# Attention and rational feed-forward: both halves of the first values in one queue, units of 6, 6 and 4 blocks, and a new order

## The chip, the cores and the metric

The kernel runs on one core of a Trainium2 chip. The metric is the device time of one execution in microseconds, taken beside other runs of the same program; three runs of the kernel before gave 272.96 (median), 270.09 and 273.46. Four engines do the work here: PE (TensorE, matrix products), DVE (VectorE), ACT (ScalarE), and POOL (GpSimd, only for constants at the start). SP issues most of the DMAs, ACT issues a few. Each engine takes its instructions strictly in the order in which the program lists them, so a wait at one instruction holds back everything listed behind it on that engine.

## What is computed

The inputs are q, k and v with 4 batches, 4 heads, 1088 positions and 32 values a head, two sketch matrices S1 and S2 of 8 by 32, and the weights of a feed-forward layer of width 2048 on 128 channels. Cut to what matters:

```python
def phi(x):                                   # 64 features from 32 values
    a = einsum('rd,bhsd->bhsr', S1, x)
    b = einsum('rd,bhsd->bhsr', S2, x)
    return einsum('bhsi,bhsj->bhsij', a, b).reshape(*x.shape[:-1], 64)
q_p, k_p = phi(q), phi(k)
kv = einsum('bhsf,bhsd->bhfd', k_p, v)
z = sum(k_p, axis=2)
x = einsum('bhsf,bhfd->bhsd', q_p, kv) / (einsum('bhsf,bhf->bhs', q_p, z)[..., None] + 1e-6)
# heads side by side: 4352 tokens of 128 channels
h = x @ w_in                                  # 4352 x 2048
P = a[0] + a[1]*h + a[2]*h**2 + a[3]*h**3
Q = 1 + abs(b[0])*abs(h) + abs(b[1])*h**2
out = (P / (Q + 1e-6)) @ w_out
```

All of the keys and values of a batch must be summed into kv before any of its queries can be finished, so the first batch's keys and values stand at the head of everything.

## The kernel before

**Attention.** For each batch, the function keys (L416) transposes the keys on DVE (L424, L426), sketches them on PE with S1 and S2 (L444), copies one of the two sketches to SBUF on ACT (L449), multiplies the two into features k_p on DVE (L452) and adds the products of k_p with the values on PE (L463). ACT keeps the sum as kvz (L480). The first batch's keys go through this in five parts of 1, 3, 2, 2 and 1 tiles. A product reads all 128 partitions of the values, which are loaded in two halves of 64 partitions (L289 and L290). The function queries (L494) transposes queries (L503), sketches them (L525 for the first two chunks, which are of 256 positions and called direct, or L553 for the others, called spread), makes features, and multiplies with kvz (L591); then come denominator, inverse and quotient on DVE (L600, L604, L607), a transpose on PE (L613) and a copy into xT on ACT (L620). The sketches of a spread chunk go out to DRAM and come back repeated over partitions (a_all and b_all, L566 to L577), before DVE multiplies them (L561). These small transfers share SP's queue with the loads.

**Feed-forward.** The 4352 tokens are cut into one tile of 256, seven of 512 and two of 256. A tile's 16 blocks of 128 hidden values are worked in units: four units of 4 blocks in the first tile, three units in each tile of 512 (PERS, L160), then units of 8, 8, and of 8, 6 and 2 blocks in the last two. There are 30 units. In each, PE computes h (L672) into one of two PSUM buffers of 1024 columns, and ACT evacuates each buffer (L676). A buffer holds two blocks of 512 tokens, so a unit with an odd number of blocks has one evacuation that is half as wide. Then DVE takes the absolute value u (L684), w = |b1| u + |b0| (DVE L689 or ACT L691) and y = w u (L694). ACT takes the logarithm (L697) and the exponential (L700): r is the inverse of the denominator. DVE makes s = h r (L709). How the polynomial is finished depends on the unit's mode, one digit of MODES (L150) a unit:

- mode 2 makes p = a3 h + a2 (L704 or L706), then h p + a1 (L718, L722 or L724) and g from it (L727); PE gathers 2 terms, r and g;
- mode 3 makes p, h s (L712) and g = p h s (L715); PE gathers 3 terms, r, s and g;
- mode 4 makes h s (L712) and h h s (L730) and no p; PE gathers 4 terms.

Each term is multiplied with a copy of the output weights that is scaled with its coefficient (L400 to L406, from the raw weights in the tile ln), and summed in PSUM (L762). DVE transposes the result (L771) and DMAs store it.

**The order.** Every step of the kernel is created with a number, and the table PLACE (L167) gives the place at which it is emitted; ON_ACT (L220) lists the steps that may run on either engine and run on ACT. Emission in the order of places fixes the order of each engine's queue. FILLS (L224) puts matmuls on idle data ahead of two places at the start. The argument behind of a DMA demands only that its place comes after that of another step; it is no wait on the chip. Buffers in PSUM and SBUF take turns (h two, hh four, r three, s, p and g two each, ln and u one), and DMAs take turns with eight semaphores: a DMA that takes a semaphore again waits first for the DMA that held it before.

**The start.** SP issues S2, the first keys, the values' first half (L289), the rest of the first queries, the two halves of the output weights, the first half of w_in, the second batch's keys and queries. ACT issues S1, the first 256 queries, the values' second half (L290) and two small loads of the vectors b and a (L308). The second half of w_in comes later on SP, between the transfers of the first spread chunk.

Of the kernel before, what the change touches and what calls it, by code (L numbers as in the profile page):

```python
# [20 lines left out]
def kernel(  # L21
# [15 lines left out]
    B, H, S, D = q.shape  # L37
# [3 lines left out]
    nf = d_ff // 128  # L41
# [8 lines left out]
    W = NT * D  # L50
# [74 lines left out]
    def d_four(n, ptr):  # L125
# [24 lines left out]
    MODES = '332423333332433332334442444442'  # L150
# [9 lines left out]
    PERS = (6, 5, 5)  # L160
# [7 lines left out]
        1, 0, 2, 3, 4, 5, 8, 13, 14, 20, 15, 73, 22, 16, 18, 6, 7, 9, 12, 10, 11, 41, 46, 59, 47, 65, 72,  # L168
        56, 82, 75, 51, 81, 85, 97, 17, 19, 24, 27, 29, 32, 21, 25, 31, 38, 26, 30, 35, 44, 33, 37, 39, 49,
        42, 45, 48, 50, 54, 23, 28, 34, 36, 52, 57, 61, 62, 66, 69, 70, 40, 53, 67, 58, 68, 74, 79, 84, 88,  # L170
        103, 111, 76, 80, 86, 87, 90, 91, 43, 60, 63, 71, 64, 89, 94, 83, 129, 132, 137, 141, 146, 149, 152,
        77, 93, 98, 105, 101, 119, 124, 127, 172, 190, 194, 200, 203, 213, 240, 106, 118, 55, 92, 96, 116,
        122, 126, 136, 120, 128, 131, 143, 104, 110, 115, 150, 166, 107, 155, 158, 162, 164, 188, 186, 173,
        216, 222, 228, 234, 237, 241, 244, 117, 176, 177, 210, 184, 218, 211, 215, 257, 263, 277, 283, 294,
        321, 344, 167, 180, 195, 196, 214, 229, 232, 267, 268, 274, 281, 284, 289, 292, 298, 278, 272, 271,
        279, 314, 319, 329, 340, 352, 370, 357, 374, 378, 387, 383, 385, 391, 402, 408, 305, 311, 317, 318,
        324, 342, 337, 338, 390, 421, 424, 428, 441, 445, 454, 347, 350, 353, 358, 356, 361, 359, 360, 407,
        468, 488, 493, 497, 510, 516, 327, 363, 366, 371, 372, 450, 418, 411, 451, 466, 487, 512, 525, 586,
        621, 457, 548, 465, 459, 483, 479, 545, 552, 566, 582, 528, 540, 565, 597, 571, 579, 580, 612, 613,
        481, 535, 539, 541, 546, 556, 561, 590, 616, 623, 626, 627, 638, 647, 654, 536, 568, 576, 588, 581,  # L180
        589, 593, 596, 660, 679, 685, 698, 703, 709, 749, 640, 650, 656, 662, 659, 674, 681, 739, 768, 787,
        793, 795, 820, 838, 840, 78, 99, 102, 108, 113, 114, 123, 134, 100, 148, 151, 135, 142, 156, 95,
        112, 121, 130, 139, 140, 153, 163, 145, 185, 189, 301, 246, 193, 125, 133, 144, 147, 154, 161, 168,
        178, 157, 174, 181, 187, 206, 239, 109, 138, 160, 165, 171, 175, 182, 192, 219, 251, 220, 221, 245,
        261, 331, 464, 431, 422, 420, 159, 170, 179, 191, 169, 183, 198, 201, 204, 212, 227, 243, 199, 209,
        223, 256, 248, 253, 250, 306, 288, 303, 202, 207, 197, 205, 208, 225, 230, 235, 238, 247, 252, 260,
        231, 266, 270, 304, 381, 259, 297, 296, 295, 302, 309, 286, 226, 236, 233, 242, 217, 224, 255, 282,
        285, 290, 299, 308, 264, 316, 323, 313, 312, 326, 325, 320, 328, 332, 335, 330, 400, 401, 410, 417,
        404, 249, 258, 254, 262, 265, 273, 291, 293, 300, 310, 322, 334, 280, 349, 369, 416, 433, 336, 396,
        379, 395, 414, 393, 415, 287, 307, 276, 333, 269, 275, 343, 348, 355, 367, 377, 386, 365, 398, 412,  # L190
        472, 437, 467, 499, 425, 443, 444, 452, 448, 315, 339, 345, 354, 341, 346, 368, 376, 382, 388, 413,
        430, 399, 434, 442, 435, 426, 485, 458, 439, 460, 449, 455, 471, 533, 663, 670, 687, 686, 752, 682,
        741, 691, 351, 362, 364, 375, 373, 384, 394, 406, 419, 429, 440, 469, 456, 477, 491, 555, 506, 482,
        519, 501, 508, 498, 504, 553, 403, 409, 389, 392, 380, 397, 432, 447, 461, 462, 490, 505, 446, 470,
        476, 527, 521, 502, 517, 530, 558, 573, 405, 423, 427, 436, 438, 453, 474, 489, 495, 500, 509, 532,
        598, 608, 549, 547, 611, 551, 538, 560, 618, 645, 646, 624, 617, 622, 649, 668, 669, 657, 653, 475,
        480, 478, 484, 486, 494, 503, 513, 514, 524, 531, 542, 522, 557, 569, 610, 543, 629, 572, 562, 564,
        603, 591, 606, 463, 473, 492, 496, 507, 515, 518, 537, 550, 559, 570, 577, 544, 585, 601, 693, 688,
        689, 609, 592, 602, 651, 643, 671, 526, 554, 511, 520, 523, 529, 575, 583, 594, 599, 630, 631, 607,
        639, 644, 633, 675, 721, 695, 642, 665, 680, 672, 692, 732, 740, 750, 756, 738, 736, 748, 734, 733,  # L200
        563, 578, 534, 567, 584, 587, 605, 614, 620, 634, 635, 664, 661, 677, 678, 655, 720, 754, 683, 711,
        725, 708, 729, 699, 574, 595, 600, 604, 615, 619, 628, 641, 652, 676, 700, 714, 684, 697, 724, 743,
        772, 716, 710, 761, 757, 764, 637, 648, 636, 658, 625, 632, 673, 696, 704, 715, 727, 735, 701, 751,
        762, 771, 742, 766, 746, 745, 782, 818, 808, 773, 825, 905, 897, 834, 909, 702, 706, 666, 690, 705,
        707, 717, 723, 728, 737, 759, 774, 718, 779, 785, 829, 812, 817, 800, 786, 797, 813, 807, 803, 713,
        722, 726, 731, 712, 719, 747, 758, 763, 775, 781, 790, 802, 819, 791, 837, 814, 799, 809, 823, 815,
        832, 824, 836, 831, 844, 730, 753, 744, 755, 667, 694, 769, 778, 784, 792, 801, 810, 835, 854, 822,
        849, 858, 839, 855, 830, 850, 868, 885, 863, 862, 856, 888, 900, 972, 906, 978, 899, 912, 894, 910,
        760, 767, 765, 776, 770, 780, 794, 796, 806, 811, 833, 847, 857, 867, 869, 908, 911, 865, 918, 866,
        892, 927, 896, 873, 880, 878, 783, 788, 777, 789, 804, 805, 826, 827, 841, 848, 859, 874, 843, 852,  # L210
        870, 879, 884, 882, 895, 914, 915, 891, 842, 846, 798, 828, 816, 821, 853, 864, 872, 876, 883, 893,
        903, 916, 919, 938, 944, 907, 917, 931, 939, 933, 942, 947, 923, 948, 960, 969, 980, 964, 970, 851,
        861, 845, 860, 877, 886, 889, 898, 904, 925, 929, 951, 924, 959, 949, 975, 956, 945, 966, 971, 875,
        890, 871, 881, 902, 913, 920, 926, 930, 941, 950, 963, 955, 967, 954, 953, 983, 962, 981, 979, 1002,
        1012, 1017, 1004, 1016, 887, 922, 901, 921, 928, 932, 934, 943, 957, 968, 977, 988, 974, 995, 991,
        1001, 985, 992, 1000, 998, 935, 936, 937, 940, 946, 952, 958, 965, 976, 989, 999, 1009, 984, 990,
# [50 lines left out]
    def flat(x, b):  # L267
        return x[b].rearrange("h (g j) d -> (h g) (j d)", g=32)
# [569 lines left out]
```

## Time and profile before

| | |
|---|---|
| time, median of 3 runs | 272.96 us (270.09 to 273.46) |
| profiled execution: its own time | 272.55 us |
| profiled execution: span from first to last instruction | 270.7 us |
| granted clock of PE, mean | 0.992 |
| busy time of ACT, share of the span | 247.6 us, 91% |
| longest wait of PE for a DMA (L463 for the values) | 2.8 us |
| longest wait of DVE (L452 for the copy L449) | 4.7 us |
| PE's waits for the evacuation L676 | 6.4 us in 13 waits, the longest 0.8 |

The profile comes from one execution. Its span leaves out 1.85 us that the execution's own time holds. A busy time is the time in which an engine had at least one instruction under way; instructions of one engine overlap a little at their ends, so durations add up to more than the busy time. A line of the timeline gives the start, the duration, the engine, the line of the code and the operation, with its output and its inputs, and in brackets how long the engine was idle before it and what released it. "x8" says that eight instructions are merged in the line. A matmul of 32-bit values counts as two instructions.

### The profile page before, as it was taken

The page shows a single profiled execution, that of the slowest core. Times are in us where ns is not written, and L with a number is a line of the kernel's source. Part 1 is how long each engine was busy: PE and PEld are TensorE (multiplying, and loading weights), DVE is VectorE, ACT ScalarE, POOL GpSimd, SP SyncE. Part 2 cuts the span into 40 slices and gives each one's busy share as a digit, 9 for nine tenths or more (in the row PEclk, how much of TensorE's full clock was granted, in tenths as well). Part 3 has the DMA queues.
Part 4 walks back from the last instruction along what each step waited for, and adds up shares of the span by engine and source line. Part 5 has one row for each costly group of instructions (what it writes and reads, how often), then busy time and mean ns, then how long its engine had stood idle before and what let it go on. Part 6 is the DMA issues. An engine that isn't in the chain of part 4 may idle for free.

```text
span 270.7 us, 4291 instructions
## 1 busy us (share of the span) xinstructions
PE 261.4 (97%) x1673; PEld 143.1 (53%) x1673; DVE 254.4 (94%) x301; ACT 247.6 (91%) x217; POOL 2.7 (1%) x25
## 2 busy tenths in 40 slices
PE   8589999999999999999999999999999999999994
PEld 5467755555443454454444554444444446666783
DVE  3389999999999999999999999999999999999993
ACT  1179999999999999999999999999998999999981
POOL 4000000000000000000000000000000000000000
PEclk9799999999999999999999999999999999999999
DMA  5947514599006447600004310430300000020032
GB/s 174 289 190 206 148 31 114 101 181 194 3 17 109 96 65 149 209 1 0 0 17 127 104 58 0 63 94 0 59 11 2 0 11 0 0 42 11 0 58 39
DMA packets 29063, 20.13 MB, mean 74 GB/s; under 512 B 19316, under 2 KB 24948, under 8 KB 29044
## 3 DMA queue, kind: packets, MB, share of 16 engines
q1 hardware_dynamic: 28064, 19.37, 31.0%
q10 hardware_dynamic: 980, 0.49, 0.7%
q8 instruction: 13, 0.21, 0.4%
q14 instruction: 6, 0.05, 0.1%
HBM read 16.65 MB, written 3.21 MB: 73 GB/s over the span
## 4 chain that ended last, share of the span: by engine, by line
PE 59%; ACT 19%; DVE 11%; issue 6%; DMA 3%; ACTq 0%; DVEq 0%
PE h_ps L672 28%; PE out_ps L762 22%; ACT ln L697 6%; ACT r L700 5%; ACT hh L676 4%; DMA v_sb<-in_v_dram 3%; PE att_ps L591 3%; ACT p L706 2%; PE att_ps L463 2%; DVE g L712 2%; PE att_ps L553 1%; PE att_ps L444 1%; DVE w L694 1%; DVE g L715 1%; DVE s L709 1%
## 5 line engine op out<-in xcount | busy, mean ns | idle before, releaser
L672 PE MATMUL h_ps<-xT,w_in_sb 128*128 128x512 f32 (+1 forms) x320 | 129.7, 537 | 0.7 <-ACT hh L676 0.3
L672 PEld LDWEIGHTS h_ps<-xT,w_in_sb 128*128 128x128 f32 x320 | 58.0, 190 | 43.8 <-issue 30.2
L762 PEld LDWEIGHTS <-w_out 128*128 128x128 bf16 x513 | 48.9, 98 | 52.5 <-issue 22.0
L676 ACT CAST hh<-h_ps 128x1024 bf16<-128x1024 f32 (+1 forms) x76 | 69.2, 949 | 1.5 <-PE h_ps L672 1.3
L697 ACT ACTIVATE ln<-w 128x2560 f32<-128x2560 bf16 (+5 forms) x30 | 65.0, 2167 | 1.0 <-DVE w L694 1.0
L700 ACT ACTIVATE r<-ln 128x2560 bf16<-128x2560 f32 (+5 forms) x30 | 65.0, 2166 | 0.4
L709 DVE TENSOR_TENSOR s<-hh,r 128x2560 bf16<-128x2560 bf16 (+5 forms) x30 | 40.8, 1360 | 0.6 <-ACT r L700 0.2
L694 DVE TENSOR_TENSOR w<-w,u 128x2560 bf16<-128x2560 bf16 (+5 forms) x30 | 40.6, 1354 | 0.1
L762 PE MATMUL out_ps<-r,w_out 128*128 128x512 bf16 (+1 forms) x160 | 39.6, 347 | 0.0
L762 PE MATMUL out_ps<-g,w_out 128*128 128x512 bf16 (+1 forms) x160 | 38.6, 347 | 0.0
L762 PE MATMUL out_ps<-s,w_out 128*128 128x512 bf16 (+1 forms) x133 | 32.3, 346 | 0.0
L706 ACT ACTIVATE p<-hh,a_sb 128x2560 bf16<-128x2560 bf16 (+3 forms) x12 | 29.2, 2431 | 0.0
L684 DVE TENSOR_SCALAR u<-hh 128x2560 uint16<-128x2560 uint16 (+5 forms) x30 | 22.7, 756 | 0.8 <-ACT hh L676 0.6
L689 DVE TENSOR_SCALAR w<-u,b_abs 128x2560 bf16<-128x2560 bf16 (+3 forms) x24 | 22.0, 919 | 0.1
L715 DVE TENSOR_TENSOR g<-p,g 128x2560 bf16<-128x2560 bf16 (+2 forms) x14 | 20.5, 1465 | 0.1
L712 DVE TENSOR_TENSOR g<-hh,s 128x2560 bf16<-128x2560 bf16 (+2 forms) x14 | 20.5, 1462 | 0.1
L712 DVE TENSOR_TENSOR p<-hh,s 128x2560 bf16<-128x2560 bf16 (+4 forms) x10 | 13.0, 1299 | 0.1
L730 DVE TENSOR_TENSOR g<-p,hh 128x2560 bf16<-128x2560 bf16 (+4 forms) x10 | 12.9, 1292 | 0.0
L762 PE MATMUL out_ps<-p,w_out 128*128 128x256 bf16 (+1 forms) x60 | 12.9, 319 | 0.0
L591 PEld LDWEIGHTS att_ps<-kvz,a_all 128*64 128x64 f32 x288 | 9.6, 137 | 5.4 <-issue 2.5
L591 PE MATMUL att_ps<-kvz,a_all 128*64 128x66 f32 x288 | 11.2, 225 | 0.6 <-DVE a_all L540 0.3
L691 ACT ACTIVATE w<-u,b_abs 128x1024 bf16<-128x1024 bf16 (+3 forms) x6 | 10.2, 1698 | 0.3 <-DVE u L684 0.3
(78 smaller groups left out, 182.2 us busy)
## 6 DMA issues: line engine op xcount, KB each, us to landing
b_all<-sk_d SPq DMA_DIRECT2D x12, 192.0 KB
a_all<-sk_d SPq DMA_DIRECT2D x6, 384.0 KB
kq<-in_k_dram SPq DMA_DIRECT2D x4, 544.0 KB
kq<-in_q_dram SPq DMA_DIRECT2D x3, 544.0 KB
a_all<-sk_d SPq DMA_DIRECT2D x4, 320.0 KB
b_all<-sk_d SPq DMA_DIRECT2D x8, 160.0 KB
v_sb<-in_v_dram SPq DMA_DIRECT2D x4, 256.0 KB
ln<-in_moe_w_out_dram SPq DMA_DIRECT2D x2, 512.0 KB
```

The costliest lines, as they stand in the source:

```text
L591: nc.tensor.matmul(nd.t[x:x + 64, o:o + 2 * KW], lhsT=(av(c)[:, o0 + x:o0 + x + 64] if how == "direct" else q_p.t[:, c * n + o0 + x:c * n ...
L672: nc.tensor.matmul(h.t[:, (x - x0) * tl:(x - x0 + 1) * tl], lhsT=w_in_sb[:, f * 128:(f + 1) * 128], rhs=xT[:, xpos(t0):xpos(t0) + tl], sta ...
L676: nc.scalar.copy(out=hh.t[:, x0 * tl:x1 * tl], in_=h.t[:, 0:(x1 - x0) * tl])
L684: nc.vector.tensor_scalar(out=u.t[:, :n].bitcast(U16), in0=hh.t[:, :n].bitcast(U16), scalar1=0x7FFF, scalar2=None, op0=AX.bitwise_and)
L694: nc.vector.tensor_mul(out=y.t[:, :n], in0=w.t[:, :n], in1=u.t[:, :n])
L697: nc.scalar.activation(out=ln.t[:, :n], in_=y.t[:, :n], func=ACT.Ln, bias=1.0 + 1e-6)
L700: nc.scalar.activation(out=r.t[:, :n], in_=ln.t[:, :n], func=ACT.Exp, scale=-1.0)
L706: nc.scalar.activation(out=p.t[:, :n], in_=hh.t[:, :n], func=ACT.Identity, scale=a3, bias=a2)
L709: nc.vector.tensor_mul(out=s.t[:, :n], in0=hh.t[:, :n], in1=r.t[:, :n])
L712: nc.vector.tensor_mul(out=(g if mode == 3 else p).t[:, :n], in0=hh.t[:, :n], in1=s.t[:, :n])
L715: nc.vector.tensor_mul(out=g.t[:, :n], in0=p.t[:, :n], in1=hs.t[:, :n])
L762: nc.tensor.matmul(o[0].t[:, :tl], lhsT=w_sb[y_][:, f0 + x, :], rhs=src.t[:, x * tl:(x + 1) * tl], start=(o[1] == 1), stop=(o[1] == o[3]))
```

## The change

There are three parts. First, both halves of the values are issued by SP, the second directly behind the first (the argument eng of load_v is gone), and the other loads of the start must have places behind the second half; the small loads of b and a only need a place behind the first queries. Second, PERS is 6, 6 and 4 blocks, and the first unit's mode is 4 instead of 3. Third, PLACE, ON_ACT and FILLS are new throughout: the table has 986 places instead of 1024. Lines behind L290 of the code move up by one.

```diff
-    MODES = '332423333332433332334442444442'
+    MODES = '432423333332433332334442444442'
...
-    PERS = (6, 5, 5)
+    PERS = (6, 6, 4)
...
     PLACE = (
-        1, 0, 2, 3, 4, 5, 8, 13, 14, 20, 15, 73, 22, 16, 18, 6, 7, 9, 12, 10, 11, 41, 46, 59, 47, 65, 72,
+        0, 1, 8, 12, 13, 28, 29, 17, 18, 70, 30, 106, 68, 48, 71, 2, 3, 5, 6, 4, 7, 40, 41, 65, 55, 85, 49,
...
     ON_ACT = (
-        24, 25, 28, 29, 32, 314, 323, 337, 379, 425, 454, 473, 502, 535, 561, 636, 655, 660, 693, 739, 879,
-        881, 990, 1008, 1013, 1015,
+        27, 28, 29, 30, 32, 328, 337, 342, 379, 423, 449, 490, 495, 525, 551, 620, 642, 672, 696, 742, 847,
+        887, 952, 970, 975, 977,
     )
-    FILLS = {7: 8, 21: 12}
+    FILLS = {3: 8, 10: 12}
...
-    def load_v(b, buf, rank, after=(), early=0.0, slack=0.3, eng=SP, behind=(None, None)):
+    def load_v(b, buf, rank, after=(), early=0.0, slack=0.3, behind=None):
         vv = v[b].rearrange("h (p s) d -> p h (s d)", p=64)
...
+        lo = dma(lambda: buf.t[0:64, :, 0:W], vv[:, :, 0:W], rank, 0.262, after, [buf], rate=300, early=early, slack=slack,
+                 behind=behind)
+        return [lo, dma(lambda: buf.t[64:128, :, 0:W + D], vv[:, :, W:2 * W + D], rank + 0.001, 0.295, after, [buf], rate=300,
+                        early=early, slack=slack, behind=lo)]
...
-    v0_l = load_v(0, v0, -203.7, slack=0.7, eng=ACTE, behind=(k0_l[0], q0_a))
+    v0_l = load_v(0, v0, -203.7, slack=0.9, behind=k0_l[0])
...
-                         eng=ACTE, cost=0.45, slack=0.7, behind=ab_in[0] if ab_in else v0_l[1]))
+                         eng=ACTE, cost=0.45, slack=0.7, behind=ab_in[0] if ab_in else q0_a))
```

The loads of both halves of w_in, of the query rest, of the second batch's keys and of the output weights each get behind=v0_l[1].

By the lists of instructions, SP now issues S2, the first keys, both halves of the values, the query rest, the first half of the output weights, the second batch's keys, the first half of w_in, the second half of the output weights and the second half of w_in, and only then the first transfers of the spread chunks. ACT issues S1 and the first queries, copies the first sketch (L449), issues b and a, and copies on; by the semaphores' turns the load of b waits for the first keys and the load of a for the values' first half. On PE both L525 sketches of the first queries and the sketch of the fourth part of the keys stand ahead of the first product L463, and the sketch of the fifth directly behind it. DVE makes the features of the second part (768 columns) before those of the first (256).

## The prediction, on record before the run

> **What bounds the kernel now.** I read the page's table of engines and its slices first, then the chain, then busy times by stretch, then the timeline of the start.
>
> ```profile
> PE 261.4 (97%) x1673; PEld 143.1 (53%) x1673; DVE 254.4 (94%) x301; ACT 247.6 (91%) x217; POOL 2.7 (1%) x25
> ```
> Three engines are nearly full; a shorter wait in the middle of one engine is soon the wait of another. The table by stretch (length, then busy us of PE, PEld, DVE, ACT, POOL, clock, DMA share, GB/s) says where the rest lies:
>
> ```profile
> 0.00:14.00 14.00, 10.14 (x86) 7.02 (x88) 4.61 (x14) 2.66 (x7) 2.74 (x25) 0.88 0.87 236
> 14.00:40.00 26.00, 25.08 (x297) 17.55 (x296) 24.89 (x54) 23.95 (x39) 0.00 (x0) 1.00 0.48 141
> 120.00:160.00 40.00, 39.88 (x230) 18.46 (x229) 39.49 (x42) 39.91 (x33) 0.00 (x0) 1.00 0.19 52
> 200.00:240.00 40.00, 39.82 (x180) 21.57 (x179) 39.96 (x37) 38.34 (x26) 0.00 (x0) 1.00 0.02 3
> ```
> DVE is idle for 9.4 us before 14.0, for about 3 us from there to 260, for 4 at the end. So the start is where time is free. The timeline there (start, us, engine, line, idle before it and its releaser):
>
> ```profile
> 7.41 1.29 DVE L452 TENSOR_TENSOR k_p<-h_ps,b_sk 128x256 f32<-128x256 f32 x2 [0.32 <-ACT b_sk L449]
> ...
> 10.88 0.70 PE L463 MATMUL out_ps<-v_sb,k_p 128*64 128x64 f32 x8 [2.76 <-DMA v_sb<-in_v_dram]
> ...
> 11.33 0.67 PE L444 MATMUL h_ps<-S,kT 128*64 128x64 f32 x8
> ...
> 11.94 1.23 PE L525 MATMUL att_ps<-qT,SAB 64*128 64x256 f32 x4
> ...
> 13.19 0.65 ACT L533 COPY a_all<-att_ps 128x256 f32<-128x256 f32 x2 [5.45 <-PE att_ps L525]
> ...
> 13.99 0.69 DVE L452 TENSOR_TENSOR k_p<-h_ps,b_sk 128x512 f32<-128x512 f32 x1 [4.69 <-ACT b_sk L449]
> ...
> 20.21 1.99 PE L672 MATMUL h_ps<-xT,w_in_sb 128*128 128x256 f32 x8
> ```
> PE stands at the first kv product (L463) until v lands at 10.85. Sketches L444 and L525, which don't need v, are queued behind it; so ACT has nothing to copy and DVE, done at 9.3, waits to 13.99. PE's first hidden matmul starts at 20.21. From there PE has no hole above 0.8 us: each L672 block of 512 columns takes 0.86 us (x8, two instructions a block, 3.44 in the chain), an L762 matmul of 512 0.215.
>
> **The loads.** The trace's transfer records show v's second half (256 packets of 1152 B, ACT's queue) dwindling to 89, 88, 49, 19 and 7 packets a us from 5 to 10, while SP's queue moves the first half, query rest and output weights. Its last packet ends at 9.82, PE wakes 1.0 later. Summed from the GB/s of 1 us stretches, 1.24 MB had moved by 7.0, 2.63 by 12, 3.30 by 14, 4.12 by 16. In the new order only 1.25 MB (keys 0.557, first queries 0.131, both halves 0.557) end with v. At the same pace: last packet 7.0 to 7.5, landed at 8.0 to 8.5. First products now need k_p of part 0, which comes second on DVE, at 8.7. So v is no longer last; DVE is.
>
> **New order of the start**, by the lists of instructions as built. PE: sketches, both halves of L525 (done 8.1 at 7.42's duration 0.70), part 3's sketch, then the first product. Part 3's sketch needs an h buffer, freed by the first k_p: one of 768 columns, 0.95, from 7.4, done 8.35. Then sketch 0.35, copy 0.23. ACT's copies stand in line before: the two small loads of the a and b vectors (0.62 and 0.26 of issue) now stand between two copies, then two L449 of 0.2, two L533 (0.65), so part 3's copy ends at about 9.4. DVE: 768, 256 and 512 wide from 7.4 end at 9.3; part 3 starts at 9.4 instead of 13.99: **4.6 us earlier.** DVE then has two a_all (0.69), two qT and part 4 (1.05), two w_out (1.34), one qT (0.43), to 13.6. PE: last product 11.6, kvz copies to 12.3, L591 0.7 behind L553 and L525, to 13.3. From 13.6 denominator, inverse and quotient take 0.6, the next a_all 0.6 beside PE's transposes and ACT's copy (0.4 each), the second L591 0.7: first hidden matmul at 15.5, **4.7 earlier** than 20.21.
>
> **What hides each load then.** The second half's issue (0.69) moves from ACT's queue to SP's; the query rest is issued 0.7 later, at 3.1, while its queue still moves keys, so that costs nothing. At the old pace the last bytes come: query rest 8.7, first half of w_out 10.6, next keys 12.4, first half of w_in 14.0, second w_out 15.2, second w_in 16.9, each plus up to 1.0 to land. Needed: 11, 11.8, 14.7, 15.5, 16.1, about 20. The first w_in has 0.5 us to spare, the second w_out (read by ACT) none; cover gone, each us late costs PE one. The read-backs of the first spread chunk now stand behind the second w_in and the next values and queries (1.6 MB): they land at some 23.5, wanted at 25.4 (28.88 less 4.6, and 1.1 us more of DVE work before it).
>
> **Added wait.** The small a load waits, by its reused semaphore, for v's first half. Behind it on ACT are four copies that DVE and PE need. First half at 6.5 to 7.5: nothing, as ACT reaches it at 7.85; if it lands as before (last packet 7.95, so 8.95), 1.1 us. I take 0, since the packets that slowed it are now queued behind; both ends stay in the range.
>
> **The clock.** PE's idle 2.76 us is followed by a halved clock (by 1 us stretches 0.84 in 10 to 11, 0.50 from 11 to 14); L525 took 1.23 instead of 0.70. No hole above 1.3 us is left in my order, so I count full clock. The Trainium skill, "TensorE: Matmul & The Clock Gate", Part 1, says the clock halves after an idle window of about 3.4 us. Here 2.76 us of visible idle was enough, so the measurement decides, and a thin window might do it.
>
> **Units 6, 6, 4, and modes.** Two half-width evacuations a tile become one: 14 of 603 ns less 7 of 1041, with 0.10 us of overlap per instruction (durations add to 269.4 on ACT, busy is 247.6): -0.5 us. Unit 0 in mode 4 drops one p (L706, 1.24) and adds four L762 of 256 (0.54). With the modes on their new sizes the sums are: ACT -0.9, DVE +0.5 (300 for 301 instructions, durations by row, 2048 and 3072 interpolated), PE three 512-column terms fewer, -0.65. ACT's 0.9 I price at nothing: it is not last.
>
> **The refit sequence.** No row shows its stalls. Along both lists I summed rows and compared, for each of the 30 units, DVE's sum before s with ACT's through r: the smallest margin goes from 2.0 to 4.7 us; for ACT's ln against y the tightest from -4.7 (start) and +1.0 (middle) to -5.9 and +0.6. So DVE's forced wait for ACT falls from about 2.6 to about 0.5, against 3 us of idle seen; at most a gain of 2. The other end is a loss: 14 units of six blocks instead of 7 hold each buffer longer. Per added six-block unit, L697 and L700 (2.80 and 2.81 against 2.38 and 2.37) are 0.86 longer before an evacuation: 7 x 0.86 = 6.0. I take 0, nearer to the summed margins.
>
> **Sum.** PE: -4.7 at the first hidden matmul, -0.65 of work: -5.35. DVE: -4.6, +0.5: -4.1. Both are full, so I take -4.8 between them. Span 270.7 to 265.9. The profiled execution took 272.55, 1.85 more than its span and 0.4 less than the median 272.96. Predicted **267.8** (1.9% under the median). Two per cent, about what can be told from no change here, is 267.5 and 278.4.
>
> **Rivals.**
> - Start gain given back: DVE has 3 us of idle in the middle and must now finish 0.5 more work in 4.7 less time; new stalls of 3 to 5 us would do. For it: three engines above 90%. Against it: the margins above. 271 to 272.5.
> - Slower: PE has two h buffers. In a six-block unit it fills both and stands until ACT ends Ln and Exp. Now this costs 6.4 us in 13 waits, the longest 0.8; 0.86 more in seven units gives 267.8 + 6.0 = 273.8, and in all 14, 279.8. It decides where PE has less than 0.86 of gathering left between two evacuations. Against it: L762 offers 90 us of such filling.
> - The clock halves again in a thin window: at 15 PE work of some 1.5 us doubles: 269.3. By the 2.76 row it might, though L553, L525 and L591 fill that stretch to over half. By the Trainium skill's rule (same page and section), an idle window, it would not.
> - The change doesn't do what it says: v lands as late as 10.8, since two queues share the engines' time before and after. Then only the sketches moved ahead of v help, or nothing: 270 to 272.4. Against it: the 1.25 MB ahead of v's end, and 2.0 by the 9.82 at which it ended before.
> - Better: the middle's idle shrinks too, -6.5: 266.
>
> Chances: forecast, 266.5 to 269.2, 0.52; better 0.10; clock 0.08; given back 0.15; late v 0.05; slower mechanism 0.10. The range, **265.3 to 273.0**, leaves out the slower one and the far end of better. Faster by over 2% (better, and the lower half of the forecast) 0.35, within 0.59, slower 0.06.
>
> **What would show it.** L463's wait for v gone or below 0.5; k_p of 512 at 9.4 to 10; the first L672 at 15 to 16; clock 1.0 from 10 to 14; DVE idle before 14 at 5 us, from there 3 or less. PE waiting on w_in_sb at 15, or its waits for L676 above 10 us, would make the prediction wrong.

## The result, and the profile after

| | kernel before | changed kernel |
|---|---|---|
| time, median of 20 executions each | 272.79 us (269.97 to 273.66) | 269.39 us (268.78 to 270.62) |
| ratio to the kernel before, 95% interval | | 0.9899 (0.9874 to 0.9923) |
| profiled execution: its own time, its span | 272.55, 270.7 us | 269.14, 267.4 us |
| first product of keys and values (L463, now L462) | 10.88 | 9.00 |
| features of part 3, 512 wide (L452, now L451) | 13.99 | 9.55 |
| first hidden matmul (L672, now L671) | 20.21 | 18.11 |
| last matmul ends | 266.9 | 263.5 |

The change makes the kernel 1.0% faster: measurable, and within 2%. Executions more than 1.5% above the fastest of their kernel beside them (four of the kernel before, beside the experiments) are left out of the ratios and averages. The time lies in the predicted range, 1.6 us above the predicted 267.8. Of the 4.8 us that the prediction expected between the two profiled spans, 3.3 came.

The page's table of engines, and the busy times by stretch with the same columns as before (length; busy us of PE, PEld, DVE, ACT, POOL; clock; DMA share; GB/s):

```profile
PE 257.5 (96%) x1672; PEld 141.7 (53%) x1672; DVE 254.1 (95%) x300; ACT 246.7 (92%) x210; POOL 2.7 (1%) x25
```

```profile
0.00:14.00 14.00, 11.11 (x148) 8.07 (x148) 8.09 (x21) 3.42 (x12) 2.74 (x25) 1.00 0.89 262
14.00:40.00 26.00, 23.96 (x268) 16.95 (x265) 23.40 (x52) 24.03 (x36) 0.00 (x0) 1.00 0.57 157
120.00:160.00 40.00, 39.55 (x208) 18.04 (x208) 40.00 (x41) 39.87 (x34) 0.00 (x0) 1.00 0.27 63
200.00:240.00 40.00, 39.62 (x163) 21.74 (x162) 40.00 (x36) 39.86 (x26) 0.00 (x0) 1.00 0.05 8
```

DVE is idle for 14 - 8.09 = 5.9 us before 14 (9.4 before the change), but for 26 - 23.40 = 2.6 us from 14 to 40 (1.1 before). From 40 to 260 its idle time falls from 1.8 to 1.0 us. The whole gain can be read on DVE: -3.5 us of idle before 14, +1.5 from 14 to 40, -0.8 from 40 to 260, -0.2 behind 260, and -0.3 of work, -3.3 in sum. The middle gave nothing back. What is short of the forecast lies before 40.

The timeline of the start of the changed kernel (start, us, engine, line; idle time and releaser in brackets):

```profile
6.64 0.26 ACTq L277 DMA_DIRECT2D ab_row<-in_moe_b_dram  x1
...
7.35 0.23 ACTq L277 DMA_DIRECT2D ab_row<-in_moe_a_dram  x1
7.62 0.18 ACT L448 COPY b_sk<-h_ps 128x32 f32<-128x32 f32 x1 [0.75 <-DMA v_sb<-in_v_dram]
...
9.00 0.45 PE L462 MATMUL out_ps<-v_sb,k_p 128*64 128x64 f32 x8 [0.35 <-DVE k_p L451]
...
9.55 0.69 DVE L451 TENSOR_TENSOR k_p<-h_ps,b_sk 128x512 f32<-128x512 f32 x1 [0.69 <-PE out_ps L462]
...
12.18 0.35 PE L385 MATMUL out_ps<-ab_row,ones 1*128 1x6 f32 x2 [1.44 <-DMA ab_row<-in_moe_a_dram]
12.46 0.92 PE L462 MATMUL out_ps<-v_sb,k_p 128*64 128x64 f32 x24
12.57 0.16 ACT L388 COPY a_sb<-out_ps 128x4 f32<-128x4 f32 x1 [2.77 <-PE out_ps L385]
12.76 1.42 DVE L403 TENSOR_SCALAR w_out<-ln,a_sb 128x1024 bf16<-128x1024 f32 x2 [0.85 <-ACT a_sb L388]
...
14.10 1.15 ACT L399 ACTIVATE w_out<-ln,a_sb 128x1024 bf16<-128x1024 f32 x1
15.15 0.57 ACT L529 COPY a_all<-h_ps 128x512 f32<-128x512 f32 x1
15.78 0.70 PE L524 MATMUL h_ps<-qT,SAB 64*128 64x256 f32 x4 [0.92 <-ACT a_all L529]
...
18.11 2.00 PE L671 MATMUL h_ps<-xT,w_in_sb 128*128 128x256 f32 x8
```

Three things are to be seen. The first product at 9.00 waits for features (0.35 us, behind DVE) and no longer for the values, whose last packet the trace's transfer records put at 7.83 (9.82 before). At 12.18 another wait has taken its place: a matmul of two instructions (L385), which spreads the polynomial's coefficients over the partitions, stands on PE ahead of the last 24 products and waits 1.44 us for the load of the vector a, 16 bytes long. ACT and DVE wait behind it (2.77 and 0.85 us). And at 14.10 ACT scales output weights for 1.15 us ahead of the copy L529, for which PE then stands (0.92 at 15.78).

### The profile page after: what moved, and what is told of

The parts are those of the page before. It is cut to its first block, busy times and chain, and to the rows that moved or that the text cites. A ratio compares the mean times of both kernels' runs of the same rounds, so it can differ in the third digit from the quotient of the medians.

```text
span 267.4 us, 4279 instructions
## 1 busy us (share of the span) xinstructions
PE 257.5 (96%) x1672; PEld 141.7 (53%) x1672; DVE 254.1 (95%) x300; ACT 246.7 (92%) x210; POOL 2.7 (1%) x25
## 4 chain that ended last, share of the span: by engine, by line
DVE 46%; PE 23%; DMA 11%; issue 9%; ACT 8%; SPq 1%; DVEq 0%; ACTq 0%
PE h_ps L671 11%; PE out_ps L761 8%; DVE s L708 7%; DVE w L693 7%; DMA b_all<-sk_d 5%; DVE u L683 4%; DVE g L714 4%; DVE g L711 3%; DVE w L688 3%; DVE g L729 3%; DVE p L711 2%; DMA sk_d<-sk_sb 2%; ACT hh L675 2%; DMA v_sb<-in_v_dram 2%; DVE g L726 2%
## 5 line engine op out<-in xcount | busy, mean ns | idle before, releaser
L671 PE MATMUL h_ps<-xT,w_in_sb 128*128 128x512 f32 (+1 forms) x320 | 128.1, 535 | 0.7 <-ACT hh L675 0.7
L671 PEld LDWEIGHTS h_ps<-xT,w_in_sb 128*128 128x128 f32 x320 | 58.4, 190 | 42.8 <-issue 30.2
L696 ACT ACTIVATE ln<-w 128x3072 f32<-128x3072 bf16 (+4 forms) x30 | 65.5, 2183 | 0.9 <-DVE w L693 0.8
L699 ACT ACTIVATE r<-ln 128x3072 bf16<-128x3072 f32 (+4 forms) x30 | 65.4, 2178 | 0.2
L693 DVE TENSOR_TENSOR w<-w,u 128x3072 bf16<-128x3072 bf16 (+4 forms) x30 | 40.7, 1356 | 0.1
L708 DVE TENSOR_TENSOR s<-hh,r 128x3072 bf16<-128x3072 bf16 (+4 forms) x30 | 40.6, 1354 | 0.0
L705 ACT ACTIVATE p<-hh,a_sb 128x3072 bf16<-128x3072 bf16 (+3 forms) x14 | 33.6, 2399 | 0.1
L688 DVE TENSOR_SCALAR w<-u,b_abs 128x3072 bf16<-128x3072 bf16 (+2 forms) x25 | 23.1, 922 | 0.1
L683 DVE TENSOR_SCALAR u<-hh 128x3072 uint16<-128x3072 uint16 (+4 forms) x30 | 22.5, 751 | 0.0
L711 DVE TENSOR_TENSOR g<-hh,s 128x3072 bf16<-128x3072 bf16 (+2 forms) x13 | 19.5, 1503 | 0.1
L714 DVE TENSOR_TENSOR g<-p,g 128x3072 bf16<-128x3072 bf16 (+2 forms) x13 | 19.5, 1501 | 0.0
L729 DVE TENSOR_TENSOR g<-p,hh 128x2048 bf16<-128x2048 bf16 (+3 forms) x11 | 13.1, 1189 | 0.1
```

The costliest lines, as they stand in the source:

```text
L671: nc.tensor.matmul(h.t[:, (x - x0) * tl:(x - x0 + 1) * tl], lhsT=w_in_sb[:, f * 128:(f + 1) * 128], rhs=xT[:, xpos(t0):xpos(t0) + tl], sta ...
L683: nc.vector.tensor_scalar(out=u.t[:, :n].bitcast(U16), in0=hh.t[:, :n].bitcast(U16), scalar1=0x7FFF, scalar2=None, op0=AX.bitwise_and)
L688: nc.vector.tensor_scalar(out=w.t[:, :n], in0=u.t[:, :n], scalar1=ab1, scalar2=ab0, op0=AX.mult, op1=AX.add)
L693: nc.vector.tensor_mul(out=y.t[:, :n], in0=w.t[:, :n], in1=u.t[:, :n])
L696: nc.scalar.activation(out=ln.t[:, :n], in_=y.t[:, :n], func=ACT.Ln, bias=1.0 + 1e-6)
L699: nc.scalar.activation(out=r.t[:, :n], in_=ln.t[:, :n], func=ACT.Exp, scale=-1.0)
```

## The experiments

The theory after the result was this: the values are mended as foreseen, and what is missing of the gain was lost in the start, at the late load of a and at the copy behind the weight scaling. The rivals: the gain comes from the order and the units and not from the queue; the two places are covered anyway; the small loads can't be earlier, because of the many pieces that SP's loads are made of; and the gain is one of PE's granted clock more than of the wait. All ratios are to the kernel before beside the experiment on the same chip. Added lines shift the numbers: L385 and L671 of the change are L386 and L672 where one line is added, L387 and L673 where two are.

### The queue alone, in the old order

On the kernel before:

```diff
-    v0_l = load_v(0, v0, -203.7, slack=0.7, eng=ACTE, behind=(k0_l[0], q0_a))
+    v0_l = load_v(0, v0, -203.7, slack=0.7, eng=SP, behind=(k0_l[0], q0_a))
```

The small loads of b and a, which stood behind the values on ACT, are thereby issued 0.7 to 1.0 us earlier (at 1.78 and 2.12); in the kernel before no engine waits for them, so this is not what the run measures.

> The kernel before with one edit: the second half of the first values is issued by SP behind the first half instead of by ACT; order, units and modes are the old ones. If the queue alone is what helps: PE's wait of 2.76 us for v falls below 0.3, no halved clock from 11 to 14, the first hidden matmul at 16.5 to 18 instead of 20.21, ratio 0.985 to 0.992, as far as the whole change. If the order written for early values is needed too: the first product waits less, but the first hidden matmul moves by under 1.5 us, and the ratio is 0.994 to 1.0.

Measured: 269.74 us, 0.9915 (0.9886 to 0.9944). The timeline:

```profile
9.22 0.45 PE L463 MATMUL out_ps<-v_sb,k_p 128*64 128x64 f32 x8 [1.04 <-DVE k_p L452]
...
11.37 0.69 DVE L452 TENSOR_TENSOR k_p<-h_ps,b_sk 128x512 f32<-128x512 f32 x1 [2.15 <-ACT b_sk L449]
...
17.54 1.99 PE L672 MATMUL h_ps<-xT,w_in_sb 128*128 128x256 f32 x8
```

One argument brings 0.85%, and the whole change 1.0%; the two intervals overlap. With the old order PE's first hidden matmul is even earlier (17.54) than in the change (18.11), though DVE gets part 3 of the keys later (11.37 against 9.55).

### The queue undone, in the new order

On the change, with the second half of the values issued by ACT again and the small loads ahead of it:

```diff
+    PLACE = PLACE[:6] + (13.3, 13.1, 13.2) + PLACE[9:]
...
-                        early=early, slack=slack, behind=lo)]
+                        early=early, slack=slack, behind=None, eng=eng)]
...
-    v0_l = load_v(0, v0, -203.7, slack=0.9, behind=k0_l[0])
+    v0_l = load_v(0, v0, -203.7, slack=0.9, behind=k0_l[0], eng=ACTE)
```

> The changed kernel with the small loads early (as in the run before, span 265.7, first hidden matmul at 17.03) and one part undone: the second half of the first values goes out on ACT's queue again, behind the first queries and the small loads. If the queue is what brings v early: its last packet comes near 9.8 again, the first product at 10.5 to 11 instead of 9.2, the first hidden matmul at 18 to 19, the span 1 to 2 us longer, ratio 0.990 to 0.994. Rival (the new order, with its sketches ahead of the first product, hides a late v, because k_p of part 4 is ready only at 11.4 in any case): first hidden matmul within 0.5 us of 17.03, ratio within 0.003 of 0.9866.

Measured: 271.02 us, 0.9956 (0.9926 to 0.9987). The values' last packet is at 9.82 again, as in the kernel before, and PE waits for it:

```profile
10.62 0.45 PE L463 MATMUL out_ps<-v_sb,k_p 128*64 128x64 f32 x8 [1.63 <-DMA v_sb<-in_v_dram]
```

Against the next experiment, which differs from it in the queue only, the queue is worth 0.9% in the new order too, as in the old one. So the late values are a matter of the two queues, and the new order, units and modes together bring 0.4% (with the small loads early, as here); the queue in the old order and the next experiment, run on one chip and both with the values on SP, lie 0.5% apart. Part of the 0.9% is PE's granted clock: the five of the twelve executions with a mean clock of 0.997 or more averaged 269.8 us, the other seven 271.3.

### The small loads early

On the change:

```diff
+    PLACE = PLACE[:7] + (13.1, 13.2) + PLACE[9:]
```

b and a are issued behind the first queries, at 1.78 and 2.13, instead of at 6.64 and 7.35 behind a copy.

> The small loads of b and a are issued directly behind the first queries; nothing else moves. Theory 1 (the load of a is what is late): in the changed kernel PE waits 1.44 us for it at 12.18, DVE then 0.85 and ACT 2.77 behind it. With the load early these waits go, kvz starts at about 12.0 instead of 13.48, the first hidden matmul at 16.5 instead of 18.11, and the span of 267.4 falls by 1.2 to 1.6 us; ratio to the kernel before about 0.984. Rival (the middle is full, so whatever the start gains is lost there again): the first hidden matmul moves, but the span falls by less than 0.5; ratio 0.988 to 0.990.

Measured: 268.19 us, 0.9866 (0.9833 to 0.9899), span 265.7.

```profile
10.89 0.38 PE L386 MATMUL out_ps<-ab_row,ones 1*128 1x6 f32 x2
...
13.01 1.15 ACT L400 ACTIVATE w_out<-ln,a_sb 128x1024 bf16<-128x1024 f32 x1
...
14.06 0.57 ACT L530 COPY a_all<-h_ps 128x512 f32<-128x512 f32 x1
14.69 0.70 PE L525 MATMUL h_ps<-qT,SAB 64*128 64x256 f32 x4 [0.92 <-ACT a_all L530]
...
17.03 1.99 PE L672 MATMUL h_ps<-xT,w_in_sb 128*128 128x256 f32 x8
```

The small matmul waits for nothing, the first hidden matmul comes 1.1 us earlier, and the span is 1.6 us shorter. The profiled execution is one of the faster of six (267.4 to 269.0 us); by the ratios the gain is 0.3%, 0.9 us. The second place shows up unchanged: the copy L530 behind the scaling L400, and PE 0.92 behind it.

### The copy ahead of the weight scaling

On the change:

```diff
+    PLACE = PLACE[:32] + (67.5,) + PLACE[33:]
```

> ACT scales the first half of the last output weight (L399, 1.15 us) behind the first copy into xT instead of ahead of the copy of the second queries' sketch (L529); the small loads stay late. Theory 2 (this step on ACT holds PE): PE's 1.06 us before its second L524 pair falls to about 0.3, the first hidden matmul comes at 17.2 to 17.5, the span falls by 0.5 to 0.9; ratio about 0.987. Rival (the weight is then missed later, or the middle is full): within 0.3 us of the changed kernel, ratio 0.989 to 0.991.

Measured: 268.83 us, 0.9906 (0.9869 to 0.9943), which can't be told from the change. In its profile the first hidden matmul is 0.8 us earlier (17.29), and the span 0.5 us shorter (266.9). The wait for a is still there (1.52), so the copy comes at 14.31 whatever stands behind it. Two of the six executions lost the full clock and took 270.6 and 270.9 us; the other four took 268.5 to 269.0.

### Both places

> Both edits. Theories 1 and 2 add: first hidden matmul at 15.5 to 16.0, which is where the prediction had it, and the span at 264.8 to 265.4; ratio 0.980 to 0.982. Rival (the middle is full): first hidden matmul as early, span not below 266.5, with more idle time of DVE or PE between 20 and 40 us. Second rival (a load is next: the first half of w_in or the second of w_out): PE or ACT waits for one of them between 14 and 17.

Both lines together gave 267.28 us, 0.9831 (0.9798 to 0.9864), span 265.3. Beside the unaltered change on one chip (further below) they gave 267.46, 0.9821 (0.9786 to 0.9855). The timeline:

```profile
8.76 0.45 PE L464 MATMUL out_ps<-v_sb,k_p 128*64 128x64 f32 x8
...
10.42 0.38 PE L387 MATMUL out_ps<-ab_row,ones 1*128 1x6 f32 x2
...
12.72 0.58 ACT L531 COPY a_all<-h_ps 128x512 f32<-128x512 f32 x1
...
15.70 1.99 PE L673 MATMUL h_ps<-xT,w_in_sb 128*128 128x256 f32 x8
```

```profile
0.00:14.00 14.00, 12.80 (x169) 9.05 (x170) 9.12 (x25) 4.20 (x13) 2.74 (x25) 1.00 0.87 259
14.00:40.00 26.00, 24.82 (x257) 16.93 (x256) 24.33 (x51) 25.31 (x36) 0.00 (x0) 1.00 0.56 161
```

The first hidden matmul is at 15.70, where the prediction had 15.5 and the change 18.11. DVE idles for 4.9 us before 14 and 1.7 from there to 40. The two places are worth 2.1 us of span, more than the 1.5 that the change lacked against the forecast (267.4 against 265.9); nothing else needs to be late. By its span this is the fastest version here, 1.7 to 1.8% under the kernel before.

### Why the small loads are late: three experiments

By the transfer records, b and a, issued at 6.64 and 7.35 in the change, are on the wire only at 11.04 and 11.39. ACT's queue holds nothing else then; SP's is full.

First, the pieces. The output weights come in 1024 pieces of 512 B for each half. In the next kernel each partition reads one piece of 4096 B, and the columns of w_in are taken with a stride of 8 so that both match:

```diff
-                moe_w_out.rearrange("(fo fi) d -> fi fo d", fi=128)[:, f0:f0 + nf // 2], WO_RANK, 0.525, (), [w_raw],
+                moe_w_out[f0 * 128:(f0 + nf // 2) * 128].rearrange("(fi fo) d -> fi fo d", fi=128), WO_RANK, 0.525, (), [w_raw],
...
-   lhsT=w_in_sb[:, f * 128:(f + 1) * 128],
+   lhsT=w_in_sb[:, f // 8 * 1024:(f // 8 + 1) * 1024].rearrange("p (i o) -> p o i", o=8)[:, f % 8],
```

> The changed kernel, with the late small loads, and one edit: within each half of the output weights a partition takes eight neighbouring rows (one piece of 4096 B) instead of eight rows 128 apart (eight pieces of 512 B), and the hidden blocks take the matching columns of w_in, every eighth. The same sums come out; the two loads are 128 pieces each instead of 1024. Theory A (the load of a, issued at 7.35 and on the wire at 11.39, waits until the 1024 pieces of the second half, issued before it, have been taken in): a is on the wire before 9, PE's wait of 1.44 us at 12.18 goes, span 265.5 to 266.5, ratio about 0.986. Theory B (ACT's queue waits its turn against SP's whatever the pieces): a still near 11, the span within 0.5 us of the changed kernel's 267.4. If columns taken eight apart slow the weight load of L671 (190 ns each), PE shows it there and the span grows by several us.

> The kernel with both edits (small loads early, L529 ahead of the weight scaling; span 265.3) and the output weights in pieces of 4096 B. If loads still held something at the start, the span falls to 264.5 or below, ratio about 0.980; if the three engines are the bound from the first hidden matmul on (15.7), it stays within 0.5 us of 265.3, ratio 0.982 to 0.984. As a version to keep it should beat both kernels of the case.

Measured: on the change 271.36 us, 0.9963 (0.9941 to 0.9984); with both places mended as well 269.96, 0.9911 (0.9881 to 0.9940). a is on the wire at 11.10 again, 3.9 us after its issue, and PE still waits for it (1.16). So the small pieces of the output weights are not what holds it. The kernel is slower by some 2 us for another reason, which the groups of instructions show (count, busy us, mean ns of one, idle us before and its releasers), first of this kernel, then of the change:

```profile
L671 PEld LDWEIGHTS h_ps<-xT,w_in_sb 128*128 128x128 f32 x320 | 90.4, 323 | 22.3 <-ACT hh L675 2.3 <-issue 0.6 <-ACT xT L619 0.4
L675 ACT CAST hh<-h_ps 128x1024 bf16<-128x1024 f32 (+1 forms) x69 | 69.3, 1030 | 3.8 <-PE h_ps L671 3.3 <-DVE g L729 0.2
```

```profile
L671 PEld LDWEIGHTS h_ps<-xT,w_in_sb 128*128 128x128 f32 x320 | 58.4, 190 | 42.8 <-issue 30.2 <-ACT hh L675 5.1 <-ACT xT L619 0.5
L675 ACT CAST hh<-h_ps 128x1024 bf16<-128x1024 f32 (+1 forms) x69 | 69.9, 1041 | 1.9 <-PE h_ps L671 1.0 <-DVE g L729 0.5
```

A weight load of 128 fp32 columns that lie 32 B apart takes 323 ns instead of 190, and ACT now waits 3.3 us for PE at the evacuations (1.0 in the change).

Second, another queue: b and a issued by SP directly behind the second half of the values.

```diff
-                         eng=ACTE, cost=0.45, slack=0.7, behind=ab_in[0] if ab_in else q0_a))
+                         eng=SP, cost=0.45, slack=0.7, behind=ab_in[0] if ab_in else v0_l[1]))
...
+    PLACE = PLACE[:7] + (29.1, 29.2) + PLACE[9:]
```

> The change, with the two small loads (b and a) issued on SP directly behind the second half of v instead of on ACT. If what counts is when they are issued and what stands ahead of them in their own queue, they are on the wire at about 7.5 to 8.5 us (11.04 and 11.39 in the change), the small product that waits for a (1.44 us in the change) waits for nothing, and the span comes out at 265.7 to 266.3 us, as with the early issue on ACT (265.7). If small loads are slow for their size whatever the queue, they go out some 4.4 us after their issue, about 10.5, and the span stays at 267.4.

Measured, in two executions: 267.73 us, 0.9827 (0.9770 to 0.9883), span 266.4. Issued at 3.05 and 3.54, b and a are on the wire at 7.87 and 7.89, while the last of the values pass, and the small matmul at 11.15 waits for nothing. From issue to wire that is 4.8 and 4.4 us, here behind the values in the same queue. So the run shows that an early issue on SP removes the wait too; it doesn't show that SP's queue is the quicker one.

Third, later on ACT: the same line with (33.1, 33.2), so that b and a are issued behind the copy of part 4 of the sketch.

> The change, with the two small loads issued on ACT later still, behind the copy of part 4 of the sketch, at about 9.1 us instead of 6.64 and 7.35. Three theories of why they reach the wire only at 11.04 and 11.39: (1) they wait for an event near 11 us, such as the end of what SP's queue holds ahead: they go out at about 11 again and the span stays at 267.4; (2) a fixed time from issue to wire of some 4.4 us in this stretch: about 13.5, the small product waits some 2 us more and the span is about 269.5; (3) the order of issue over both queues decides: they go out behind the second w_in load, at 16 or later, and the span is 272 or more.

Measured: 271.88 us, 0.9990 (0.9951 to 1.0029), span 270.5. Issued at 8.72 and 9.02, they are on the wire at 12.41 and 12.64: later than in the change, so they don't wait for an event at 11, and ahead of the second half of w_in, whose issue began at 6.02 and whose pieces pass until 17.6, so it is not the order of issue over both queues either. What agrees in all these kernels is a time of 3.6 to 4.4 us from issue on ACT to the wire while SP's queue is full (2.5 to 3.1, once 3.8, when issued at 1.8 to 2.1 behind the first queries). What it is made of stays open.

The load of a comes 1.25 us later, and the span grows by 3.1 us. Where the rest comes from is seen in the timeline and in the clock by stretches of 1 us (the seventh figure behind the colon that is not in brackets):

```profile
13.72 0.56 PE L386 MATMUL out_ps<-ab_row,ones 1*128 1x6 f32 x2 [3.27 <-DMA ab_row<-in_moe_a_dram]
14.21 1.55 PE L463 MATMUL out_ps<-v_sb,k_p 128*64 128x64 f32 x24
```

```profile
12.00:13.00 1.00, 0.00 (x0) 0.00 (x0) 0.00 (x0) 0.00 (x0) 0.00 (x0) 0.87 1.06 381
13.00:14.00 1.00, 0.28 (x2) 0.31 (x2) 0.00 (x0) 0.00 (x0) 0.00 (x0) 0.50 1.11 303
...
19.00:20.00 1.00, 1.00 (x9) 0.28 (x6) 0.64 (x2) 0.00 (x0) 0.00 (x0) 0.72 0.00 0
```

PE waits 3.27 us, and then works at half clock to 19.6; the 24 products take 1.55 us instead of 0.92.

### The change itself once more, and the clock

> The change itself once more, on the same chip as the version with both places mended: span 267.4 us, 0.990 of the kernel before.

> The change with the small loads early and the copy of the state ahead of the weight scaling, once more, on the same chip as the change itself. If these two places took what the forecast missed, the span is 265.3 us, 0.983 of the kernel before and 0.7% below the change; if the earlier difference lay between chips, the two agree within 0.3%.

Measured on one chip: the change 269.80 us (269.34 to 270.05), 0.9901 (0.9869 to 0.9932); both places mended 267.46 (267.28 to 267.93), 0.9821. The six executions of the one and the six of the other don't overlap, and the medians lie 0.9% apart. But the second profile of the same kernel is not the first:

```profile
12.35 0.35 PE L385 MATMUL out_ps<-ab_row,ones 1*128 1x6 f32 x2 [1.71 <-DMA ab_row<-in_moe_a_dram]
12.63 1.18 PE L462 MATMUL out_ps<-v_sb,k_p 128*64 128x64 f32 x24
```

```profile
12.00:13.00 1.00, 0.65 (x14) 0.66 (x16) 0.06 (x1) 0.16 (x1) 0.00 (x0) 1.00 1.07 399
13.00:14.00 1.00, 1.00 (x24) 0.84 (x19) 1.00 (x2) 0.09 (x1) 0.00 (x0) 0.56 1.10 311
14.00:15.00 1.00, 1.00 (x8) 0.51 (x4) 0.79 (x2) 0.96 (x4) 0.00 (x0) 0.50 1.16 328
15.00:16.00 1.00, 1.00 (x14) 0.68 (x14) 0.00 (x0) 1.00 (x2) 0.00 (x0) 0.50 0.91 330
16.00:17.00 1.00, 1.00 (x14) 0.62 (x10) 0.41 (x3) 0.15 (x1) 0.00 (x0) 0.74 0.27 85
```

The wait for a was 0.27 us longer here, and the clock halved behind it; the first hidden matmul came at 18.79 instead of 18.11, the span at 267.7 instead of 267.4. So the clock does halve in the change too, in some executions, though behind the wait for a and not in the thin window near 15 that the prediction named. The mean clock of every execution shows how often. The kernel before has 68 counted executions beside the experiments (the last one included): 12 at 0.997 or more, 270.7 us on average; 39 at 0.990 to 0.994, 272.0 us; 17 below that, 273.2 us. Of the change's 26 executions, 16 had 0.997 or more (269.5 us on average), 9 had 0.990 to 0.994 (269.6 us), one 0.987. With both places mended all 10 had 0.997 or more.

One step of the mean clock is one stretch of 3.4 us at half clock: 3.4 / 2 / 270 = 0.006. The stretches by 1 us add up to that length: in the last table (0.44 + 0.50 + 0.50 + 0.26) x 2 = 3.4 us, in the kernel with the later loads twice that.

The clock records of the traces say when a wait does this. The clock changes only at steps of 3.41 us from the moment at which it became full (6.29 in the change's second profile, where it halves at 13.12, two steps later). In the step just ahead of the halving PE was idle for 1.71 us there, 2.55 in the kernel before and 2.29 with the later loads; in the change's first profile PE was idle for 1.64 us of such a step, with the copy first for 1.67, and the clock stayed full. So in these five profiles it turns near half of a step, and how the wait falls on the steps decides as well as its length. The executions agree: of the kernels in whose profile PE waits 1.16 us at most, all 57 kept 0.997 or more; the change did in 16 of 26, the copy first (a wait of 1.52) in 4 of 6, the queue undone (1.63) in 5 of 12, the kernel before (2.76) in 12 of 68, the later loads (3.27) in none of 8.

### The kernel before, kept warm

If the clock makes those steps, matmuls on idle data ahead of the first product should take them out of the kernel before, with the values as late as ever:

```diff
-    FILLS = {7: 8, 21: 12}
+    FILLS = {7: 8, 21: 12, 32: 20}
```

> The kernel before with one line changed: 20 matmuls on idle data (about 0.107 us each at full clock, 2.1 us in all) ahead of the first product of keys and values, where PE otherwise stands 2.76 us for the second half of v. The values land as late as before (PE still waits for them until about 10.8); only the halved clock behind the wait can go. Of 55 executions of the kernel before beside the earlier experiments, 9 had a mean granted clock of 0.997 or more and averaged 270.6 us, 29 had 0.990 to 0.994 and averaged 272.0, 17 were below 0.99 and averaged 273.3. If the clock makes these steps, nearly all executions of this kernel have 0.997 or more, the median is 270.6 us, 1.5 us or 0.6% below the kernel before, and L525 and the products behind the wait take 0.70 and 0.92 us instead of 1.23 and 1.35. If the clock is only a sign of something else (the values later in those executions, for instance), the median stays at 272 to 273 us.

Measured: 271.19 us, 0.9972 (0.9947 to 0.9996); all twelve executions had a clock of 0.997 or more.

```profile
7.84 2.36 PE L330 MATMUL out_ps<-idle 128*128 128x256 bf16 x20
...
10.63 0.45 PE L463 MATMUL out_ps<-v_sb,k_p 128*64 128x64 f32 x8 [0.43 <-DMA v_sb<-in_v_dram]
10.88 0.43 PE L444 MATMUL h_ps<-S,kT 128*64 128x64 f32 x8
11.24 0.70 PE L525 MATMUL att_ps<-qT,SAB 64*128 64x256 f32 x4
11.87 0.92 PE L463 MATMUL out_ps<-v_sb,k_p 128*64 128x64 f32 x24
...
18.94 1.99 PE L672 MATMUL h_ps<-xT,w_in_sb 128*128 128x256 f32 x8
```

The values come at 10.6, as before. L525 takes 0.70 us instead of 1.23, the products 0.92 instead of 1.35, and the first hidden matmul comes 1.3 us earlier in the profile, the last one too (it ends at 265.6 against 266.9). In the medians it is 0.8 us; the interval holds 0.1 to 1.4, so the expected 1.5 was too much. On this chip the three executions of the kernel before that kept the clock averaged 271.0 us, about the 271.2 of the warm kernel. The clock is a cause by itself, but the smaller part: the queue alone gave 0.85%, warmth alone 0.3%.

## Why the prediction was right, and where it was not

**The bound, and the values.** Right. The start was where time was free. The first product at 9.0 with no wait for the values, part 3 of the features at 9.55 (9.4 predicted), the values' last packet at 7.83, 0.3 later than the 7.0 to 7.5 worked out. The rival in which the values stay late was built as an experiment, the queue undone: 271.02 us, in its range of 270 to 272.4.

**The order of the start on PE.** Here the prediction failed. Its step "PE: last product 11.6, kvz copies to 12.3 ... first hidden matmul at 15.5" summed the products and left out two instructions that are in its own lists: the small matmul of a ahead of the last products, and the weight scaling on ACT ahead of the copy L529. For the loads of b and a it counted what their issue takes on ACT, and never when they land. The last products began at 12.46 and the first hidden matmul at 18.11. With both mended, 15.70 was measured and a span of 265.3, where the sum had 265.9. So the size of the step was right for an order that the change does not have. The measured 269.39 lies in the stated range, but above the 266.5 to 269.2 that the prediction gave to its own forecast. The range took in a loss that no rival had named, and in that the prediction had luck.

**"Added wait", taken at 0, bounds 0 to 1.1.** It was 0.75 us of ACT before the copy at 7.62, where ACT waited for the values' first half. The bounds held it; the price at the end can't be told apart from that of the late load itself, since moving the loads removes both.

**The clock.** Full in the profiled execution of the change, as counted, and in 16 of its 26 executions. "No hole above 1.3 us" did not hold, since the wait for a was 1.44 and 1.71 in the two profiles. The waits for a DMA ahead of the products that kept the full clock were 1.44, 1.52 and 1.63 us; those that lost it were 1.71, 2.76 and 3.27. Each is one profiled execution, and other executions of the first three kernels lost it. The Trainium skill, "TensorE: Matmul & The Clock Gate", Part 1, has a free-running window of about 3.4 us, so that where the idle time falls in it matters: the length of the halved stretches here, 3.4 and 6.8 us, agrees. Its threshold, a whole idle window, does not: 1.71 us of idle time in a step was enough. The prediction's price for this rival, 1.5 us, was too high for the change: its executions with one step less of clock were only 0.2 us slower, while in the kernel before a step is 1.3 us, and with the copy first 2.0. In its second profile 0.3 of the 0.7 us by which the first hidden matmul was later reached the end; which other wait hid the rest wasn't followed further.

**The base.** The profiled execution before had a clock of 0.992, so the sum of -4.7 for the first hidden matmul held some 1.3 us of clock (the warm kernel's 18.94 against 20.21) without saying so. That was no error of the sum, but the median of the kernel before moves with the share of its executions that lose the clock. The sum also stands beside the profiled execution and leaves out the 0.4 us by which, as it says, that one lay under the median; with them it gives 268.2.

**Units, modes and sequence, taken at 0 in all.** ACT's work fell by 0.9 us (247.6 to 246.7), as worked out, and it was not last. DVE's fell by 0.3 where +0.5 was forecast. No run separates the units from the new sequence; together, on DVE, they are worth about the 1.3 us that the result's account shows behind 40 and in the work. The slower rival, PE standing while ACT ends logarithm and exponential, did not come: its waits for the evacuation fell from 6.4 us in 13 to these:

```profile
PEld h_ps L671 <- ACT hh L675: 5.1, 9, 0.8
```

(total us, times, the longest, from the table of waits). Nor was the gain given back in the middle: 1.8 us of DVE idle between 40 and 260 became 1.0. The loads' margins held: no engine waits for w_in or w_out. The read-back of the first spread chunk held too, but that of the second, which the prediction did not look at, was late, as the timeline shows:

```profile
33.31 0.82 DVE L560 TENSOR_TENSOR a_all<-a_all,b_all 128x640 f32<-128x640 f32 x1 [0.94 <-DMA b_all<-sk_d]
```

That is 0.9 of the 1.5 us by which DVE's idle time grew between 14 and 40. With the small loads early it is 0.4, with both places mended it is gone, where the read-backs are issued at 25.7 instead of 27.7.

**"What would show it."** The wait for v, the features at 9.4 to 10 and the clock came as written; DVE's idle before 14 was 5.9 instead of 5, from there 3.6 instead of 3 or less, and the first hidden matmul missed its 15 to 16. This list would have led straight to the failing step.

## What to carry to other kernels

When a late transfer is mended, list all that the instructions behind the wait read, however small: here 16 bytes, issued 5 us too late behind a copy, took back 1.6 us of span in the profiles and 0.9 us by the ratios. Issue tiny constants first, ahead of the bulk. A wait on TensorE can be dearer than its length, since the clock may halve behind it: look at the granted clock of many executions, not of one, and where the wait can't go, matmuls on idle data in it bring part of the time back.

## What was not expected of the hardware

- A load of 8 or 16 bytes on ACT's queue, which held nothing else, was on the wire 3.6 to 4.4 us after its issue while SP's queue was full, whether the output weights on SP had pieces of 512 or of 4096 B. The Trainium skill, "DMA: Bandwidth & Descriptors", "Queues, rings and completion order", has each engine go round between the queues packet by packet, a packet being several pieces. By that alone such a load would be out after about one packet of the other queue; whether a packet here can take 4 us, no run shows.
- Halves of one transfer in two queues end later than in one, as the prediction had counted on: the second half's last packet at 9.75 to 9.82 on ACT's queue in three kernels, at 7.72 to 8.70 behind the first half on SP's.
- Weights of fp32 read with a stride of 8 elements load in 323 ns instead of 190. The Trainium skill, "TensorE: Matmul & The Clock Gate", "LDWEIGHTS (loading the stationary operand)", lets the time go by the columns alone, which are 128 in both; here the stride counts as well.
- The times of the kernel before fall into steps of some 1.3 us, by how many stretches of 3.4 us at half clock an execution has, and the clock halves when PE was idle for about half of a step of 3.41 us (1.71 us lost it, 1.67 kept it).
